# A windowed-attention and mixer kernel: the second period written out as a fixed list, and the global sums moved to the head of each period

## The chip, the cores and the metric

The kernel runs on one core of one Trainium2 chip. The time of a kernel is device microseconds (us) of one execution. TensorE (PE in the profile) multiplies matrices and writes to PSUM; VectorE (DVE) and ScalarE (ACT) read PSUM and do elementwise work; GpSimd (POOL) and SyncE (SP) issue transfers here, and GpSimd does some copies at the start. Every engine works through its own instructions strictly in the order in which the program lists them, and waits where an instruction needs something that is not ready.

## The reference, cut to what matters

For each of 8 batches, 8 heads of 576 positions and width 64 go through attention in which a position sees those within 32 of it and 8 global positions (and the global positions see all). The heads are joined to `x` (576 by 512), and a mixer follows: a token step and a channel step.

```
scores = where(|i - j| <= 32 or i global or j global, q @ k.T / 8, -1e9)
x = softmax(scores) @ v                        # heads joined: 8 x 576 x 512
u = x + (relu(x.T @ w_tok1) @ w_tok2).T        # 576 -> 256 -> 576
out = u + relu(u @ w_ch1) @ w_ch2              # 512 -> 1536 -> 512
```

## The kernel before

Batch 0's attention and token step stand at the start, written out instruction by instruction. After that comes a loop over b = 0 to 7. I call one turn a period. Period b does the channel step of batch b ("dense" work) and, between its parts, the attention and token step of the next batch, n = b + 1, and the first part of the attention of the batch after that, m = b + 2 ("sparse" work). The tile framework is in manual scheduling: each engine's order is the order in which the program calls the steps.

`dense(b)` is a list of units: 12 times `M4` (a channel product of four 128x512 matmuls into PSUM tile `b1p`, whose ReLU is taken by ScalarE at line 758), for odd b three `M4l` (`b1lp`: the last 64 rows of two batches together), and then `M5` in halves of six matmuls (`op`, line 781; VectorE adds the residual at line 785 into `osb`, and SyncE sends it out).

The sparse steps of a batch, with their names in the profile:

- `TR` and `t` = `T` + `TE`: transposes of q and k (`pr`, `pT`), copied out by VectorE (lines 438, 406, 412); one `T` for each of four head pairs. `globals_` copies the global queries (line 392).
- `s2(b, p)`: band scores of a head pair (`s`, line 458), exponentials by ScalarE (line 470); `SM`: masks on VectorE, first the eight global columns into `eg` (line 476), then the band (line 481, twice).
- `GK`: scores with the global queries (`gk`), exponentials (lines 527, 528), mask (`lf`, line 532).
- `OG`: the global positions' sums (`og`, line 539). It reads `eg` of all four head pairs, so it needs the first instruction of the last `SM`. VectorE copies it out as `rf` (line 544).
- `v_odd`: two copies on VectorE (`vod`, lines 373 and 374) of v shifted by 64 rows.
- `PV(b, tau)`: the output of attention for 128 positions (`pv`, lines 656 and 665); it begins with `rf`, and VectorE divides at lines 678 and 679 into `x`.
- `M1`: token product 1 (`a1p`), ReLU on ScalarE (line 700; batch 1: lines 697, 698); `M2`: token product 2 (`hp`), residual on VectorE (lines 721, 724) into `u` and `ul`; `M3`: transposes of `u` by DMA on SyncE's queue (`uT`), or, for batch 1, `M3p` on TensorE (`pu`, line 745; copied out at line 747). `uT` is what `M4` of that batch reads.
- `casts`: ten conversions of the loaded q and k of batch m on ScalarE (lines 383, 386), in pairs.

PSUM tiles come from three pools: `psm` (two buffers: `b1p`, `b1lp`, `op` and some of the transposes), `pss` (two larger buffers: scores, half of `pv`, `a1p`, `hp`) and `psv` (one large buffer: `gk`, `og`, the other `pv`). A new tile waits until the engine that reads the old one in its buffer is done.

The order of the two kinds of work is set in two ways. `play(steps, d)` runs a fixed list, in which an entry `D` stands for "the next dense unit". `merge(sparse, dense)` deals the two lists out by cost weights. Period 0 is a fixed list `period_0` (it ends, once its 20 dense units are used up, in a stretch of sparse steps alone: `M3p`, `M2(1, 2)`, and the first transposes and scores of batch 2). Period 1 is `merge(sparse2(), units)`. Periods 2 to 7 are `first_half(b)` with the `M4` units and `second_half(b)` with the `M5` units; `second_half` ends with `OG` of the next batch but one.

Of the kernel before, what the change touches and what calls it, by code (L numbers as in the profile page):

```python
# [9 lines left out]
F16 = mybir.dt.float16  # L10
# [5 lines left out]
P = 128  # L16
# [28 lines left out]
def kernel(  # L45
# [342 lines left out]
    def casts(b):  # L388
        return [lambda ti=ti, p=p: cast_qk(b, ti, p, nc.scalar.copy) for p in (None, 0, 1, 2, 3) for ti in range(2)]
# [4 lines left out]
        )  # L394

    def T(b, p):
        pT = (psm if b in (0, 2) else psv if b == 1 or p % 2 else pss)([P, 2, 512], F16, name=f"pT_{b}_{p}")
        for ti, n in enumerate((qn, kn)):
            for i in range(4):
                nc.tensor.transpose(  # L400
                    out=pT[:, ti, P * i : P * i + P], in_=n[b % 2][:, i, 2 * p : 2 * p + 2, :], identity=ident
                )
        st[b]["pT", p] = pT
# [15 lines left out]
        TEk(b, p)  # L419

    def TR(b):
        pr = (psm if b in (0, 2) else psv)([P, 2, 4, NP * 16], name=f"pr_{b}")
        sel = ident.rearrange("p (n r x) -> p r n x", n=NP, r=2)
        for ti, n in enumerate((qr, kr)):
            for i in range(4):
                for par in range(2):
                    nc.tensor.matmul(
                        pr[64 * par : 64 * par + 64, ti, i, :], lhsT=n[b % 2][:, i, :], rhs=sel[:, par], start=True, stop=True
                    )
        st[b]["pr"] = pr  # L430
        if b > 0:
            TRE(b)
# [74 lines left out]

    def GK(b):
        s = st[b]
        ps = (psv if b != 2 else pss)([P, 2, 512], name=f"gk_{b}")  # L510
        for p in range(NP):
            o = ps[32 * p : 32 * p + 32]
            qv = qTs[b % 2][:, p, :, NG:QS]
            w = kgz[:, b, p, :]
            nc.tensor.matmul(o[:, 0, 0:384], lhsT=w, rhs=qv[:, 0:3], start=True, stop=True)
            nc.tensor.matmul(o[:, 1, 0:128], lhsT=w, rhs=qv[:, 3], start=True, stop=True)
            nc.tensor.matmul(o[:, 1, 128:192], lhsT=w, rhs=qv[:, 4, 0:LAST], start=True, stop=True)
        s["gk"] = ps
# [14 lines left out]

    def OG(b):
        s = st[b]
        ps = (psv if b != 2 else pss)([P, 2, VW], name=f"og_{b}")
        for c in range(NT):
            for p in range(NP):
                nc.tensor.matmul(
                    ps[32 * p : 32 * p + 32], lhsT=eg[:, c, 2 * p : 2 * p + 2, :],  # L540
                    rhs=vsh[b % 2][:, c, 2 * p : 2 * p + 2, :], start=(c == 0), stop=(c == NT - 1),
                )
        rf = mb.tile([P, NP, 2, VW], F16, tag="rf", name=f"rf_{b}")
        nc.vector.tensor_tensor(
            out=rf, in0=ps.unsqueeze(1).to_broadcast([P, NP, 2, VW]),
            in1=blk.rearrange("p (n r) -> p n r", r=2).unsqueeze(3).to_broadcast([P, NP, 2, VW]), op=ALU.mult,
        )
        s["rf"] = rf
# [98 lines left out]
    def PV(b, tau):  # L647
# [145 lines left out]
        T(b, p)  # L793
        TE(b, p)

    def sparse2():
        b, n = 2, 3
        cs = casts(n)

        def cast(k):  # L800
            return [(0.0, c) for c in cs[2 * k : 2 * k + 2]]

        u = [(0.0, lambda: (load_rest(n), load_qk(n, slice(0, H))))]
        u += [(1.0, s2(b, 1)), (0.0, lambda: SM(b, 1)), (1.0, lambda: t(b, 3)), (1.5, s2(b, 2)), (0.0, lambda: SM(b, 2)), (0.0, lambda: v_odd(b))]
        u += [(0.3, lambda: GK(b)), (0.3, lambda: S_(b, 3, 0)), (1.8, lambda: S_(b, 3, 1)), (0.0, lambda: SM(b, 3))]
        u += [(2.5, lambda: OG(b))]
        u += [(2.0, lambda: PV(b, 0)), (2.0, lambda: PV(b, 1)), *cast(0), (2.0, lambda: PV(b, 2)), *cast(1)]
        u += [(0.0, lambda: PV(b, 3)), (1.0, lambda: [M1(b, ch) for ch in range(3)]), *cast(2)]
        u += [(2.0, lambda: PV(b, 4)), *cast(3), (3.0, lambda: [M1(b, ch) for ch in range(3, NT)]), *cast(4)]
        u += [(0.0, lambda: (load_rest(n + 1), load_qk(n + 1, slice(0, H))))]  # L810
        u += [(0.0, lambda: load_v16(n))]
        u += [(1.3, lambda: (M2(b, 0), M3(b, 0))), (1.0, lambda: (M2(b, 1), M3(b, 1)))]
        u += [(2.0, lambda: (M2(b, 2), M3(b, 2) if b % 2 else None))]
        u += [(1.0, lambda: (globals_(n), TR(n)))]
        u += [(1.2, lambda p=p: t(n, p)) for p in range(NP)]
        for p in range(NP):
            u += [(0.3, lambda p=p: S_(n, p, 0)), (2.2, lambda p=p: S_(n, p, 1)), (0.0, lambda p=p: SM(n, p))]
            if p == 2:
                u += [(0.5, lambda: GK(n)), (0.0, lambda: v_odd(n))]
        return u  # L820
# [14 lines left out]
    def period_0():  # L835
        n, m = 1, 2
        D = None
        c2 = casts(m)
        c1 = [lambda ti=ti, p=p: cast_qk(1, ti, p, nc.scalar.copy) for p in (2, 3) for ti in range(2)]
        u = [D, D, D, D, D, D, lambda: TR(n), lambda: globals_(n), D, lambda: t(n, 0), *c1[:2], D]  # L840
        u += [lambda: t(n, 1), *c1[2:], lambda: (load_qk1(2), load_v16(2)), D, s2(n, 0), D, lambda: t(n, 2), lambda: SM(n, 0), D, s2(n, 1), D]
        u += [lambda: t(n, 3), lambda: SM(n, 1), s2(n, 2), lambda: v_odd(n), D, lambda: SM(n, 2), lambda: GK(n), s2(n, 3), D]
        u += [lambda: SM(n, 3), lambda: OG(n), D, lambda: PV(n, 0), lambda: PV(n, 1), D, lambda: PV(n, 2), lambda: PV(n, 3), D]
        u += [*c2, lambda: PV(n, 4), lambda: [M1(n, ch) for ch in range(NT - 1)], D, lambda: M1(n, NT - 1), lambda: globals_(m), D]
        u += [lambda: M2(n, 0), lambda: M2(n, 1), lambda: TR(m), D, lambda: M3p(n, 0), lambda: t(m, 0)]
        u += [lambda: M3p(n, 1), lambda: (M2(n, 2), M3(n, 2)), lambda: t(m, 1)]
        u += [s2(m, 0), lambda: t(m, 2), lambda: SM(m, 0)]
        return u

        return u  # L850

    def first_half(b):
        n, m = b + 1, b + 2
        D = None
        cs = casts(m) if m < B else []

        def c(k):
            return cs[2 * k : 2 * k + 2]

        def tt(p):  # L860
            return [lambda: t(m, p)] if m < B else []

        def pv(tau):
            return lambda: PV(n, tau)

        if n == B:
            return []
        u = [D, *([lambda: OG(n)] if b == 2 else []), D, pv(0), pv(1), *c(0), D, *c(1), D, pv(2), pv(3), *c(2), D, lambda: [M1(n, ch) for ch in range(3)], D]
        if b == 2:
            u += [lambda: gather_t(1)]  # L870
        u += [pv(4), *c(3), D, lambda: M1(n, 3), D, *([lambda: TR(m)] if m < B else []), lambda: M1(n, 4), *c(4)]
        if m < B:
            u += [lambda: load_v16(m), lambda: globals_(m)]
        if m + 1 < B:
            u += [lambda: (load_rest(m + 1), load_qk(m + 1, slice(0, H)))]
        u += [D, *tt(0), D, lambda: (M2(n, 0), M3(n, 0)), D, *tt(1), lambda: (M2(n, 1), M3(n, 1)), D, *tt(2)]
        u += [lambda: (M2(n, 2), M3(n, 2) if n % 2 else None), D]
        return u

    def second_half(b):  # L880
        m = b + 2
        D = None
# [195 lines left out]
```

## Time and profile before

| | |
|---|---|
| median of 5 runs | 334.48 us (333.73 to 335.51) |
| the profiled execution | 332.79 us, its span from first to last instruction 330.7 us |
| TensorE clock granted, mean | 0.997 |
| busy: TensorE, VectorE, ScalarE, GpSimd | 310.9, 190.8, 155.2, 62.5 us |
| chain that ended last: share on TensorE, VectorE | 78%, 16% |

The shares are averages over stages that are bound by different things, and the end of a matmul in the profile is modelled. So the useful view is a stretch of the timeline, engine by engine, and what is read from it is start to start: the time from the start of one step to the start of the next. A bracket at the end of a line names the idle time of the engine ahead of it and who ended it. Period 0 begins at about 36 us, period 1 at about 78, period 2 at about 121, and the later ones follow every 35 to 38 us.

### The profile page before, as it was taken

How to read it: one execution, taken by the hardware profiler on the slowest of the kernel's cores; microseconds unless marked ns; L12 is line 12 of the kernel's file. 1: busy time of each engine (PE TensorE's matmuls, PEld its weight loads, DVE VectorE, ACT ScalarE, POOL GpSimd, SP SyncE). 2: the span in 40 equal slices, each digit the busy share in tenths (PEclk: the TensorE clock that was granted, in tenths of full speed). 3: DMA queues.
4: the chain of work that ended last, by engine and by line, in shares of the span. 5: the costliest groups of instructions: out<-in, count | busy, mean ns of one | idle time of the engine just before them, and what ended most of it. 6: DMA issues, size and time to landing. Idle time of an engine off the chain costs nothing.

```text
span 330.7 us, 8236 instructions
## 1 busy us (share of the span) xinstructions
PE 310.9 (94%) x3505; PEld 171.2 (52%) x3505; DVE 190.8 (58%) x414; ACT 155.2 (47%) x281; POOL 62.5 (19%) x95
## 2 busy tenths in 40 slices
PE   4999997997999999999999999999999999999994
PEld 4768544544455545454556445544556445444641
DVE  7378469669644875577736574577636574431021
ACT  3561685336665166625574326725673423504600
POOL 5796569410040004000310004000000000000000
PEclk9999999999999999999999999999999999999998
DMA  7899998995696919493589419593003111051012
GB/s 226 193 152 226 279 186 213 226 113 113 225 92 139 257 66 116 46 295 113 83 55 294 90 65 113 81 268 107 34 0 65 66 64 34 14 131 63 2 73 86
DMA packets 78198, 41.85 MB, mean 127 GB/s; under 512 B 54482, under 2 KB 72274, under 8 KB 78162
## 3 DMA queue, kind: packets, MB, share of 16 engines
q0 software_dynamic: 38608, 12.88, 32.1%
q1 hardware_dynamic: 39552, 28.45, 31.9%
q8 instruction: 27, 0.44, 0.5%
q14 instruction: 9, 0.07, 0.1%
q10 hardware_dynamic: 2, 0.00, 0.0%
HBM read 36.11 MB, written 9.44 MB: 138 GB/s over the span
## 4 chain that ended last, share of the span: by engine, by line
PE 78%; DVE 16%; ACT 2%; issue 2%; DVEq 0%; ACTq 0%
PE op L781 25%; PE b1p L755 22%; PE a1p L692 5%; PE hp L716 4%; PE pv L656 3%; PE b1lp L768 3%; PE pT L400 3%; PE s L458 3%; PE pv L665 3%; PE warm L208 2%; DVE vod L373 2%; DVE vod L374 2%; DVE e_all L481 2%; DVE kT L412 1%; DVE qT L406 1%
## 5 line engine op out<-in xcount | busy, mean ns | idle before, releaser
L755 PE MATMUL b1p<-uT,wc 128*128 128x512 f16 x384 | 94.9, 380 | 0.8 <-ACT b L758 0.6
L758 ACT ACTIVATE b<-b1p 128x512 f16<-128x512 f32 x96 | 57.0, 599 | 76.6 <-PE b1p L755 76.6
L781 PE MATMUL op<-wc,b 128*128 128x512 f16 x384 | 90.0, 380 | 0.0
L470 ACT ACTIVATE e_all<-s 128x544 f16<-128x544 f32 (+1 forms) x64 | 40.9, 685 | 38.4 <-issue 26.0
L755 PEld LDWEIGHTS <-wc 128*128 128x128 f16 x384 | 34.9, 98 | 39.8 <-issue 2.2
L781 PEld LDWEIGHTS <-b 128*128 128x128 f16 x384 | 35.1, 98 | 39.0
L361 POOL DMA_DIRECT2D vsh<-in_v_dram x35 | 29.7, 854 | 133.4 <-DVE rr L678 115.9
L785 DVE TENSOR_TENSOR osb<-u,op 128x512 f32<-128x512 f16 x32 | 21.9, 686 | 53.1 <-PE op L781 51.0
L678 DVE RECIPROCAL rr<-pv 128x8 f32<-128x8 f32 (+1 forms) x35 | 7.1, 203 | 30.9 <-PE pv L665 30.9
L679 DVE TENSOR_TENSOR x<-pv,rr 128x512 f16<-128x512 f32 (+1 forms) x35 | 24.2, 691 | 1.2
L481 DVE TENSOR_TENSOR e_all<-e_all,bandm 128x616 f16<-128x616 f16 x56 | 24.3, 475 | 1.0
L406 DVE COPY qT<-pT 128x512 f16<-128x512 f16 x30 | 20.5, 685 | 6.7 <-PE pT L400 6.2
L721 DVE TENSOR_TENSOR u<-x,hp 128x1024 f16<-128x1024 f16 x14 | 17.0, 1217 | 12.1 <-PE hp L716 12.1
L412 DVE COPY kT<-pT 128x512 f16<-128x512 f16 x30 | 20.4, 680 | 1.9 <-PE pT L400 1.4
L716 PE MATMUL hp<-a,w 128*128 128x512 f16 x72 | 19.1, 378 | 1.4 <-DVE u L721 1.3
L656 PE MATMUL pv<-rf,lf 128*64 128x264 f16 x126 | 18.3, 283 | 0.9 <-DVE kgz L355 0.7
L386 ACT CAST kn<-lk 128x512 f16<-128x512 f32 x27 | 16.8, 621 | 2.6 <-DMA lk<-in_k_dram 2.6
L665 PE MATMUL pv<-vsh,e_all 128*64 128x66 f16 x280 | 18.0, 194 | 0.0
L386 ACT CAST qn<-lq 128x512 f16<-128x512 f32 x27 | 16.5, 613 | 3.1 <-DMA lq<-in_q_dram 3.1
L665 PEld LDWEIGHTS <-e_all 128*64 128x64 f16 x504 | 17.9, 111 | 0.0
L458 PE MATMUL s<-qT,kT 64*64 64x136 f16 (+2 forms) x704 | 16.3, 216 | 1.2 <-DVE ul L724 0.7
L458 PEld LDWEIGHTS <-kT 64*64 64x64 f16 x704 | 10.8, 107 | 12.6 <-issue 10.9
(175 smaller groups left out, 354.2 us busy)
## 6 DMA issues: line engine op xcount, KB each, us to landing
out_dram<-osb SPq DMA_DIRECT2D x32, 256.0 KB
lq<-in_q_dram SPq DMA_DIRECT2D x5, 1024.0 KB
lk<-in_k_dram SPq DMA_DIRECT2D x5, 1024.0 KB
wc<-in_moe_w_ch_dram POOLq DMA_DIRECT2D x6, 512.0 KB, 13.5
vsh<-in_v_dram POOLq DMA_DIRECT2D x21, 128.0 KB, 4.5
lq<-in_q_dram POOLq DMA_DIRECT2D x2, 1024.0 KB
lk<-in_k_dram POOLq DMA_DIRECT2D x2, 1024.0 KB, 13.1
vsh<-in_v_dram POOLq DMA_DIRECT2D x14, 96.0 KB, 4.4
```

What stands on the lines that cost most here:

```text
L361: nc.gpsimd.dma_start(out=vsh[b % 2][r0:r1, c, :, 0:D], in_=v[b, :, j0 : j0 + (r1 - r0), :].rearrange("h p d -> p h d"),)
L386: eng(out=(qn, kn)[ti][b % 2][:, :, hs].rearrange("p i h d -> p h i d"), in_=(lq, lk)[ti][:, hs])
L458: nc.tensor.matmul(ps[o, par, i0 - a : i1 - a], lhsT=kT[r, HQ * j : HQ * j + HQ], rhs=qf[r, i0:i1], start=b > 0, stop=b > 0 or j in js[-2:],)
L470: nc.scalar.activation(out=e2[:, :, a:z], in_=ps[:, :, 0 : z - a], func=AF.Exp, scale=scale)
L481: nc.vector.tensor_mul(out=e2[:, par], in0=e2[:, par], in1=bm)
L656: nc.tensor.matmul(ps[r0 : r0 + 64, hf, 0 : NP * VW], lhsT=s["lf"][:, HQ * t : HQ * t + HQ], rhs=s["rf"][:, 2 * hf : 2 * hf + 2], start=Tr ...
L665: nc.tensor.matmul(ps[r0 : r0 + 64, hf, VW * hh : VW * hh + VW], lhsT=e_all[:, h, lo : lo + HQ], rhs=(vod if t % 2 else vsh)[b % 2][:, tau ...
L679: nc.vector.tensor_tensor(out=x16s[b % 2][r, tau, :].rearrange("p (f h x) -> p f h x", f=2, h=NP), in0=pq[r, :, :, 0:D], in1=rr[r].unsquee ...
L716: nc.tensor.matmul(ps[:, i, :], lhsT=w2[:, ch, P * tau - sh : P * tau - sh + P], rhs=s["a1"][:, ch, :], start=(ch == 0), stop=(ch == 1),)
L755: nc.tensor.matmul(ps, lhsT=wc1[:, cc, P * j : P * j + P], rhs=s["uT"][:, cc, :], start=(cc == 0), stop=(cc == 3))
L758: nc.scalar.activation(out=s["b1"][:, j, :], in_=ps, func=AF.Relu)
L781: nc.tensor.matmul(ps, lhsT=w, rhs=wc2[:, j, :], start=(j == 0), stop=(j == NJ - 1))
```

## The change

Period 1 becomes a fixed list, `period_1`, which begins after `M3p(1, 1)`: the last steps of `period_0` move into it, with channel products of batch 1 between them. `sparse2` goes. `OG` moves from the end of `second_half` to the head of `first_half`, behind one channel product. In `second_half`, `v_odd` moves from the place after `GK` to the place before the third `SM`; in `period_0`, from before the third `SM` to after the fourth. In `first_half` the casts and some dense units change places: in particular the token ReLU of `M1(n, 4)` now comes behind the last pair of casts, and one channel product fewer stands between `M1(n, 4)` and `M2(n, 0)`. Some PSUM tiles of batches 1 and 2 change pool.

```diff
     def T(b, p):
-        pT = (psm if b in (0, 2) else psv if b == 1 or p % 2 else pss)([P, 2, 512], F16, name=f"pT_{b}_{p}")
+        pT = (psm if b == 0 or (b, p) in ((2, 0), (2, 2), (1, 1)) else psv if b < 3 or p % 2 else pss)([P, 2, 512], F16, name=f"pT_{b}_{p}")
...
-        pr = (psm if b in (0, 2) else psv)([P, 2, 4, NP * 16], name=f"pr_{b}")
+        pr = (psm if b in (0, 2) else pss if b == 1 else psv)([P, 2, 4, NP * 16], name=f"pr_{b}")
...
-        ps = (psv if b != 2 else pss)([P, 2, 512], name=f"gk_{b}")
+        ps = psv([P, 2, 512], name=f"gk_{b}")
...
-        ps = (psv if b != 2 else pss)([P, 2, VW], name=f"og_{b}")
+        ps = psv([P, 2, VW], name=f"og_{b}")
...
-        ps = (pss if b != 2 and tau % 2 else psv)([P, 2, 512], name=f"pv_{b}_{tau}")
+        ps = (pss if tau % 2 else psv)([P, 2, 512], name=f"pv_{b}_{tau}")
...
-    def sparse2():
...
     def period_0():
...
-        u += [lambda: t(n, 3), lambda: SM(n, 1), s2(n, 2), lambda: v_odd(n), D, lambda: SM(n, 2), lambda: GK(n), s2(n, 3), D]
-        u += [lambda: SM(n, 3), lambda: OG(n), D, lambda: PV(n, 0), lambda: PV(n, 1), D, lambda: PV(n, 2), lambda: PV(n, 3), D]
+        u += [lambda: t(n, 3), lambda: SM(n, 1), s2(n, 2), D, lambda: SM(n, 2), lambda: GK(n), s2(n, 3), D]
+        u += [lambda: SM(n, 3), lambda: v_odd(n), lambda: OG(n), D, lambda: PV(n, 0), lambda: PV(n, 1), D, lambda: PV(n, 2), lambda: PV(n, 3), D]
...
-        u += [lambda: M3p(n, 1), lambda: (M2(n, 2), M3(n, 2)), lambda: t(m, 1)]
-        u += [s2(m, 0), lambda: t(m, 2), lambda: SM(m, 0)]
+        u += [lambda: M3p(n, 1)]
         return u
...
+    def period_1():
+        n, m = 2, 3
+        D = None
+        c3 = casts(m)
+        u = [D, lambda: (M2(1, 2), M3(1, 2)), D, lambda: t(n, 1), lambda: (load_rest(m), load_qk(m, slice(0, H))), D, s2(n, 0), D]
+        u += [lambda: t(n, 2), lambda: SM(n, 0), D, s2(n, 1), D, lambda: t(n, 3), lambda: SM(n, 1), D, s2(n, 2), lambda: v_odd(n), D]
+        u += [lambda: SM(n, 2), lambda: GK(n), D, s2(n, 3), D, lambda: SM(n, 3), lambda: OG(n), *c3[0:2], D, D, lambda: PV(n, 0)]
+        u += [lambda: PV(n, 1), *c3[2:4], D, *c3[4:6], D, lambda: PV(n, 2), lambda: PV(n, 3), *c3[6:8], D]
+        u += [lambda: [M1(n, ch) for ch in range(3)], *c3[8:10], D, lambda: PV(n, 4), lambda: load_v16(m), D, lambda: M1(n, 3)]
+        u += [lambda: TR(m), lambda: M1(n, 4), lambda: (load_rest(m + 1), load_qk(m + 1, slice(0, H))), lambda: globals_(m), D, lambda: t(m, 0), D]
+        u += [lambda: (M2(n, 0), M3(n, 0)), D, lambda: t(m, 1), lambda: (M2(n, 1), M3(n, 1)), D, lambda: t(m, 2), D, lambda: M2(n, 2)]
+        u += [lambda: t(m, 3), s2(m, 0), D, lambda: SM(m, 0), s2(m, 1), D, lambda: SM(m, 1), s2(m, 2), D, lambda: SM(m, 2), lambda: GK(m)]
+        u += [D, s2(m, 3), lambda: v_odd(m), lambda: SM(m, 3), D]
         return u
...
     def first_half(b):
...
-        u = [D, *([lambda: OG(n)] if b == 2 else []), D, pv(0), pv(1), *c(0), D, *c(1), D, pv(2), pv(3), *c(2), D, lambda: [M1(n, ch) for ch in range(3)], D]
+        u = [D, lambda: OG(n), *c(0), D, D, pv(0), pv(1), *c(1), D, *c(2), D, pv(2), pv(3), D, lambda: [M1(n, ch) for ch in range(3)], *c(3), D]
         if b == 2:
             u += [lambda: gather_t(1)]
-        u += [pv(4), *c(3), D, lambda: M1(n, 3), D, *([lambda: TR(m)] if m < B else []), lambda: M1(n, 4), *c(4)]
+        u += [pv(4), D, lambda: M1(n, 3), *c(4), D, *([lambda: TR(m)] if m < B else []), lambda: M1(n, 4)]
...
-        u += [D, *tt(0), D, lambda: (M2(n, 0), M3(n, 0)), D, *tt(1), lambda: (M2(n, 1), M3(n, 1)), D, *tt(2)]
-        u += [lambda: (M2(n, 2), M3(n, 2) if n % 2 else None), D]
+        u += [*tt(0), D, lambda: (M2(n, 0), M3(n, 0)), D, *tt(1), lambda: (M2(n, 1), M3(n, 1)), D]
+        u += [*tt(2), lambda: (M2(n, 2), M3(n, 2) if n % 2 else None)]
         return u

     def second_half(b):
...
-        return [D, s2(m, 0), D, lambda: t(m, 3), lambda: SM(m, 0), D, s2(m, 1), D, lambda: SM(m, 1), D, s2(m, 2), D,
-                lambda: SM(m, 2), lambda: GK(m), lambda: v_odd(m), s2(m, 3), D, lambda: SM(m, 3), D, lambda: OG(m)]
+        return [D, s2(m, 0), D, lambda: t(m, 3), D, lambda: SM(m, 0), s2(m, 1), D, lambda: SM(m, 1), D, s2(m, 2), lambda: v_odd(m), D, lambda: SM(m, 2),
+                lambda: GK(m), s2(m, 3), D, lambda: SM(m, 3), D]
...
         if b == 1:
-            merge(sparse2(), units)
+            play(period_1(), units)
             continue
```

More of the change, by code (lines that the diff above doesn't have):

```diff
@@ L794, in t @@
         TE(b, p)
-    def sparse2():
[L797 to L820, printed above, removed]
     def play(steps, d):
@@ L841, in period_0 @@
         u += [lambda: t(n, 1), *c1[2:], lambda: (load_qk1(2), load_v16(2)), D, s2(n, 0), D, lambda: t(n, 2), lambda: SM(n, 0), D, s2(n, 1), D]
-        u += [lambda: t(n, 3), lambda: SM(n, 1), s2(n, 2), lambda: v_odd(n), D, lambda: SM(n, 2), lambda: GK(n), s2(n, 3), D]
-        u += [lambda: SM(n, 3), lambda: OG(n), D, lambda: PV(n, 0), lambda: PV(n, 1), D, lambda: PV(n, 2), lambda: PV(n, 3), D]
+        u += [lambda: t(n, 3), lambda: SM(n, 1), s2(n, 2), D, lambda: SM(n, 2), lambda: GK(n), s2(n, 3), D]
+        u += [lambda: SM(n, 3), lambda: v_odd(n), lambda: OG(n), D, lambda: PV(n, 0), lambda: PV(n, 1), D, lambda: PV(n, 2), lambda: PV(n, 3), D]
         u += [*c2, lambda: PV(n, 4), lambda: [M1(n, ch) for ch in range(NT - 1)], D, lambda: M1(n, NT - 1), lambda: globals_(m), D]
         u += [lambda: M2(n, 0), lambda: M2(n, 1), lambda: TR(m), D, lambda: M3p(n, 0), lambda: t(m, 0)]
-        u += [lambda: M3p(n, 1), lambda: (M2(n, 2), M3(n, 2)), lambda: t(m, 1)]
-        u += [s2(m, 0), lambda: t(m, 2), lambda: SM(m, 0)]
-        return u
+        u += [lambda: M3p(n, 1)]
+        return u
+        return u
+    def period_1():
[11 more added lines that the diff above has]
+        u += [D, s2(m, 3), lambda: v_odd(m), lambda: SM(m, 3), D]
         return u
```

## The prediction

> **What bounds the kernel now.** I read the page's first two parts, then TensorE's waits, then the timeline of each period engine by engine.
>
> ```profile
> PE 310.9 (94%) x3505; PEld 171.2 (52%) x3505; DVE 190.8 (58%) x414; ACT 155.2 (47%) x281; POOL 62.5 (19%) x95
> ...
> PEclk9999999999999999999999999999999999999998
> ```
>
> TensorE sets the pace and has its full clock everywhere. The change leaves its work alone (as many matmuls, in another order), so it can only win or lose TensorE's waits and the turn between kinds of tile. Its listed waits are few:
>
> ```profile
> PE og L539 <- DVE eg L476: 2.6, 3, 1.7
> ...
> PE hp L716 <- DVE u L721: 1.3, 4, 0.3
> PE s L458 <- DVE ul L724: 0.7, 1, 0.7
> ...
> PE b1p L755 <- ACT b L758: 0.6, 2, 0.4
> ```
>
> Modelled matmul ends hide more, so I take start to start. Full-speed prices from undisturbed places: M4 0.86 us, an op half 1.29, M4l 0.90, T 0.45, s2 0.40 and GK 0.38 (each 0.1 more behind a wide matmul), OG 0.46, two PV in a row 1.19, one alone 0.70, M1 0.43 a step, M2 0.86, 0.86 and 0.43. What a reader needs of the lags: a reader of PSUM starts about 0.2 behind the last matmul (0.27 for the token ReLU), TensorE 0.06 behind the reader's end.
>
> The join of two periods shows where TensorE waits although no bracket says so. VectorE and TensorE at the end of period 2:
>
> ```profile
> 151.65 0.87 DVE L481 TENSOR_TENSOR e_all<-e_all,bandm 128x616 f16<-128x616 f16 x2
> 153.91 0.69 DVE L785 TENSOR_TENSOR osb<-u,op 128x512 f32<-128x512 f16 x1 [1.39 <-PE op L781]
> ...
> 156.01 0.71 DVE L373 COPY vod<-vsh 64x2112 f16<-64x2112 f16 x1
> 156.75 0.70 DVE L374 COPY vod<-vsh 64x2112 f16<-64x2112 f16 x1
> 157.37 0.18 DVE L476 TENSOR_TENSOR eg<-e_all,egm 128x80 f16<-128x80 f16 x1
> ...
> 158.38 0.68 DVE L785 TENSOR_TENSOR osb<-u,op 128x512 f32<-128x512 f16 x1
> ```
>
> ```profile
> 157.27 0.80 PE L539 MATMUL og<-vsh,eg 128*32 128x132 f16 x20
> 158.00 2.13 PE L755 MATMUL b1p<-uT,wc 128*128 128x512 f16 x8
> 160.06 0.30 PE L656 MATMUL pv<-rf,lf 128*64 128x264 f16 x2
> ```
>
> OG holds TensorE for 0.73 instead of 0.46, because eg comes at 157.55 behind the v copy. The two channel products take 2.06 instead of 1.82, because the second needs the buffer that osb frees at 159.06. And VectorE had idled 1.39 us earlier.
>
> **The change part by part.**
>
> *Batch 1's pools (period 0).* pT_1 waited 0.61 for pT_0's copy; in psm it doesn't, but the next M4 then waits for the ReLU of M4 number 7, done at 44.68: it starts at 44.75 instead of 44.94. Gain 0.19. pr in pss costs nothing: that pool is free until the first scores.
>
> *v copy of batch 1 behind the last masks.* Before, VectorE is full from 50.48 on:
>
> ```profile
> 52.81 0.71 DVE L373 COPY vod<-vsh 64x2112 f16<-64x2112 f16 x1
> 53.55 0.95 DVE L374 COPY vod<-vsh 64x2112 f16<-64x2112 f16 x1
> ...
> 55.80 0.68 DVE L785 TENSOR_TENSOR osb<-u,op 128x512 f32<-128x512 f16 x1
> 56.39 0.19 DVE L476 TENSOR_TENSOR eg<-e_all,egm 128x80 f16<-128x80 f16 x1
> ...
> 57.41 0.70 DVE L544 TENSOR_TENSOR rf<-og,blk 128x528 f16<-128x528 f32 x1
> ```
>
> Without the copy (1.6 us) the masks come earlier, but osb needs op, whose end is at 54.23, and starts only at 54.45. So: osb to 55.05, eg at 55.24, masks to 56.07, copy to 57.5, rf to 58.2. OG no longer waits 1.75; PV waits for rf instead and starts at 58.26 (58.43 before). What is late next: the casts of batch 2, behind lk's landing, hold ScalarE until the token ReLU starts at 67.81, whatever TensorE does:
>
> ```profile
> 67.29 0.61 ACT L386 CAST kn<-lk 128x512 f16<-128x512 f32 x1
> 67.81 0.59 ACT L697 ACTIVATE a<-a1p 128x512 f16<-128x512 f32 x1
> ```
>
> So both edits end here: between 0 and 0.2 gained; I take 0.
>
> Here a rule speaks against the change. The copies now stand at 56.1 to 57.5, among five v loads that GpSimd issues from 54.00 to 58.30. The row: a copy beside GpSimd's issuing took 0.71 (52.81) and 0.95 (53.55), against 0.70 with GpSimd idle (156.75), so 0.25 more at most. The Trainium skill (SBUF — State Buffer, Who interferes with whom) says that a two-port copy on VectorE and GpSimd lock each other out of a shared pair of ports for a whole instruction. By the row PV starts up to 0.25 later and the cast limit swallows most. By the rule the copy could be shut out until 58.30: rf at 60.4, PV 2.0 later, about 1.85 lost. I take the row; the rule sets the far end.
>
> *The head of period 1.* M4 number 0 now stands right behind pu and reads all of uT. VectorE copies the last part of it at 75.46 to 75.88, behind q and k of pT_0, so TensorE waits from 74.64 to 75.95: 1.31. Before, M2, T and half of s2 filled this.
>
> I carried period 1 on by hand in this manner, queue by queue. Other waits of the new list: M4 number 4, 0.68 (its buffer's ReLU queues behind a pair of exponentials that ends at 81.24); OG of batch 2, 0.82 (exponentials of the last scores end at 90.1, eg follows); s2 of batch 3, 0.20 (ul); OG of batch 3, 1.99. The last is fixed by VectorE: from the end of the last op half, 0.22 + osb 0.60 + SM 1.02 + mask 0.48 + v copy 1.36 + eg 0.18 + 0.06 = 3.9 us, while TensorE has only GK, s2 and one M4 (1.8). Sum 5.00. The same reckoning of the old list, with its waits read from the trace (0.73, 0.50, 0.50, 0.29, 0.35, 0.17, 0.17, 0.14, 0.05, 0.73, 0.17): 3.80. The new list saves turns: four single PV become two pairs, 2.80 to 2.38; three scores are no longer split, 0.12 each. Net +1.20 - 0.42 - 0.36 = +0.42. It isn't seen in the trace, so it has ends: -2.5 (half of the new waits don't come) and +2.
>
> Hidden in it: SyncE sends q and k of batch 4 and out ahead of uT of batch 2. The loads' bytes flow about 7 us behind their issue (102.9 before, 105.3 now), and transposes follow: done at 114.3 before, 116.7 now by the same 11.4. M4 of period 2 comes at 120.5. The 3.8 us between are the cover; each us beyond costs one. q and k of batch 3 are issued some 1.5 us later and land by 90; casts start at 90.5. GpSimd's v loads wait for PV as before, a period ahead.
>
> *Joins of periods 2 to 5.* The v copy (1.45) fits into VectorE's idle 1.39 before osb, which moves 0.1. eg and osb come early, OG stands behind an M4: 0.27 saved at four joins, 0.24 at the two even ones (behind an odd period the last op tile leaves room). Sum -1.56. If a v copy still delayed osb there, TensorE wouldn't feel it: op's buffer has 3 us.
>
> *Token ReLU in first_half.* The row of period 6, which has no sparse work to hide in:
>
> ```profile
> 283.18 0.59 PE L692 MATMUL a1p<-x,w1l 128*128 128x512 f16 x2
> 283.87 1.02 ACT L700 ACTIVATE a<-a1p 128x1024 f16<-128x1024 f32 x1
> 285.33 1.03 PE L716 MATMUL hp<-a,w 128*128 128x512 f16 x4
> ```
>
> From the end of a1p the ReLU takes 0.27 + 1.02 + 0.06 = 1.35. Before, two M4 (1.73) covered it. Now one M4 (0.86): 0.49, say 0.50, lost in period 6. In periods 2 to 5, T and M4 (1.31) cover it: 0.04 each, 0.16. The casts ahead of it end in time (ScalarE is free at 3.09 after M4 number 7 starts, a1p's lag ends at 3.32).
>
> *Nothing:* the 0.3 waits of hp for u stay, their order is the same; gather_t stays next to PV; periods 6 and 7 beyond the ReLU are unchanged.
>
> **Sum:** 0 + 0.42 - 1.56 + 0.50 + 0.16 = -0.48, say -0.5. The profiled execution (332.79, of which the span is 330.7 and 2.1 lie around it) would be 332.3; it ran 1.7 under the median, so I put the change onto the median: 334.0.
>
> **The rivals.** What a measurement tells from no change is about 0.3%, 1.0 us.
>
> - A, forecast: waits change places, 334.0, own range 333.2 to 334.6. Chance 0.46, of which 0.10 lies beyond -1.0.
> - B, faster: the fixed list avoids half its 5.0 us of new waits, -0.5 - 2.5 = 331.5. For it: ScalarE has 0.5 to 1 us to spare between most of its steps. Against it: the 1.31 and the 1.99 follow from VectorE's order alone. 0.24.
> - C, slower: the port lock at batch 1's v copy, +1.85 - 0.48 = 335.85. Place: 56.1 us; it decides from a delay of 1.6 on (0.1 swallowed by the casts, 0.5 by the gain elsewhere, 1.0 to count). Against it: 0.71 and 0.95 in the row. 0.15.
> - D, slower: in period 1 a ReLU behind exponentials holds M4 not once but at each of the four score pairs, 3 x 0.68 more: 336.0. Against it: 1.0 us of margin at the other three. 0.10.
> - E: the change doesn't do what it says, since uT's transposes land late and period 2 waits; at 5.5 us late, 335.7. 0.05.
>
> Faster: 0.10 + 0.24 = 0.34. Same: 0.36, from A. Slower: C, D and E, 0.30. The range takes in B's centre and A, and reaches C: 331.5 to 335.8.
>
> **What would show it.** In the profile after: no wait of 1.7 at og near 55, but PV right behind rf at 58.2 to 58.5; a wait of 1.3 at the first b1p at 75.9; og near 121.4 cut by 2 us; OG at the later joins 0.46 long behind a b1p, v copies in VectorE's former gap; hp in period 6 waiting 0.5 for ScalarE. Wrong it would be if periods 2 to 5 don't shorten by 0.3 to 0.5 each, or if period 1 takes over 1 us more or less.

## The result, and the profile after

The changed kernel took 334.09 us (median of 42 runs, 331.85 to 338.47), the kernel before 335.06 us (79 runs beside them). The ratio is 0.9975, with a 95% interval of 0.9958 to 0.9991: faster by 0.84 us, of which the interval allows 0.3 to 1.4. The forecast was 334.0, a gain of 0.48. (Ratios leave disturbed runs out; the medians given with the experiments hold all runs, so the two need not agree to the last tenth.)

The profiled execution took 331.87 us, its span is 330.1. I first look at the page's busy times and at TensorE's waits, to compare them with those shown of before:

```profile
PE 308.3 (93%) x3505; PEld 170.7 (52%) x3505; DVE 192.3 (58%) x414; ACT 155.7 (47%) x281; POOL 62.3 (19%) x95
...
PEclk9999999999999999999999999999999999999998
```

```profile
PE og L539 <- DVE eg L476: 3.1, 3, 1.8
...
PE hp L716 <- DVE u L721: 1.3, 4, 0.3
PE pv L656 <- DVE rf L544: 1.2, 1, 1.2
PE b1p L755 <- DVE uT L747: 1.1, 1, 1.1
PE b1p L755 <- ACT b L758: 1.0, 2, 0.5
...
PE hp L716 <- ACT a L700: 0.3, 1, 0.3
```

As many instructions on every engine, the same clock. The list of waits has become longer, not shorter, although the time is less: `b1p` now waits for `uT`, `pv` for `rf`, `hp` for the token ReLU, and `og` waits more. All four were named ahead of the result. What the list can't show is what went away, since it stood in no bracket. For that the stages are needed.

I cut the timeline of TensorE into stages, start to start. *Period 0* runs from the first `b1p` to the second `pu` of batch 1, *period 1* to the first `pv` of batch 3, *periods 2 to 5* to the first `pv` of batch 7, *period 6* to the first `hp` of batch 7. The new `first_half` has one M4 more ahead of a `pv`, so for kernels with it I take 0.86 from period 1 and add it to period 6. Behind the last stage TensorE has some 40.5 us more to do in every kernel.

| kernel | first `b1p` at | period 0 | period 1 | periods 2 to 5 | period 6 |
|---|---|---|---|---|---|
| before | 35.79 | 38.41 | 50.68 | 148.39 | 12.06 |
| after | 37.07 | 38.02 | 50.67 | 146.49 | 12.52 |
| difference | +1.28 | -0.39 | -0.01 | -1.90 | +0.46 |
| e1_joins | 37.02 | 38.45 | 50.54 | 146.49 | 12.52 |
| e2_list | 36.52 | 38.76 | 51.79 | 148.83 | 12.06 |
| e3_vcopy | 37.83 | 38.71 | 50.68 | 148.41 | 12.06 |
| e4_v_early | 36.21 | 39.31 | 49.54 | 146.50 | 12.53 |
| e5_relu6 | 37.56 | 38.13 | 52.35 | 146.49 | 12.05 |
| e6_head | 35.90 | 38.72 | 49.83 | 146.51 | 12.52 |
| e7_all_waits | 37.03 | 38.23 | 48.01 | 146.49 | 12.05 |
| e8_hp_late | 37.32 | 38.54 | 48.00 | 144.51 | 12.05 |
| e9_buffers | 39.22 | 37.99 | 46.62 | 144.52 | 12.05 |

Rows e5 and e2 hold a fall of the granted clock, and period 0 of e1 to e4 and e6 a score pair that stood longer; both are told below. The gain comes from the joins of periods 2 to 5. At the join whose waiting was shown of before, TensorE's timeline of after reads:

```profile
158.08 1.03 PE L755 MATMUL b1p<-uT,wc 128*128 128x512 f16 x4
159.04 0.47 PE L539 MATMUL og<-vsh,eg 128*32 128x132 f16 x20
159.44 1.90 PE L755 MATMUL b1p<-uT,wc 128*128 128x512 f16 x8
161.27 0.30 PE L656 MATMUL pv<-rf,lf 128*64 128x264 f16 x2
```

and VectorE's:

```profile
151.72 0.69 DVE L785 TENSOR_TENSOR osb<-u,op 128x512 f32<-128x512 f16 x1 [0.64 <-PE op L781]
...
153.45 0.71 DVE L373 COPY vod<-vsh 64x2112 f16<-64x2112 f16 x1
154.19 0.70 DVE L374 COPY vod<-vsh 64x2112 f16<-64x2112 f16 x1
154.82 0.68 DVE L785 TENSOR_TENSOR osb<-u,op 128x512 f32<-128x512 f16 x1
...
157.13 0.20 DVE L476 TENSOR_TENSOR eg<-e_all,egm 128x80 f16<-128x80 f16 x1 [0.26 <-ACT e_all L470]
```

OG now holds TensorE for 159.44 - 159.04 = 0.40 (0.73 before), and the two channel products for 1.83 (2.06 before). The v copies lie in the gap in which VectorE had idled for 1.39, and eg comes as soon as the exponentials allow, 1.7 us and more ahead of need.

### The profile page after: what moved, and what is told of

Its sections match the earlier page's. It is cut to its first block, busy times and chain, and to the rows that moved or that the text cites. A ratio compares the mean times of both kernels' runs of the same rounds, so it can differ in the third digit from the quotient of the medians.

```text
span 330.1 us, 8234 instructions
## 1 busy us (share of the span) xinstructions
PE 308.3 (93%) x3505; PEld 170.7 (52%) x3505; DVE 192.3 (58%) x414; ACT 155.7 (47%) x281; POOL 62.3 (19%) x95
## 4 chain that ended last, share of the span: by engine, by line
PE 74%; DMA 12%; DVE 6%; SPq 3%; ACT 2%; issue 1%; POOL 1%; POOLq 0%; ACTq 0%
PE op L781 28%; PE b1p L755 21%; DMA wc<-in_moe_w_ch_dram 8%; PE a1p L692 5%; PE hp L716 4%; PE b1lp L768 3%; PE pv L656 3%; PE pv L665 3%; PE s L458 3%; PE pT L400 2%; DMA lq<-in_q_dram 2%; DMA lk<-in_k_dram 2%; DVE u L721 1%; DMA lv<-in_v_dram 1%; SPq L128 1%
## 5 line engine op out<-in xcount | busy, mean ns | idle before, releaser
L470 ACT ACTIVATE e_all<-s 128x544 f16<-128x544 f32 (+1 forms) x64 | 40.5, 687 | 35.5 <-issue 16.4
```

The source lines that it names most:

```text
L470: nc.scalar.activation(out=e2[:, :, a:z], in_=ps[:, :, 0 : z - a], func=AF.Exp, scale=scale)
```

## The experiments

**e1_joins: the halves alone.** The kernel before, with `first_half` and `second_half` of after; `period_0`, the merged period 1 and the pools stay.

```diff
-        u = [D, *([lambda: OG(n)] if b == 2 else []), D, pv(0), pv(1), *c(0), D, *c(1), D, pv(2), pv(3), *c(2), D, lambda: [M1(n, ch) for ch in range(3)], D]
+        u = [D, lambda: OG(n), *c(0), D, D, pv(0), pv(1), *c(1), D, *c(2), D, pv(2), pv(3), D, lambda: [M1(n, ch) for ch in range(3)], *c(3), D]
...
```

> Only first_half and second_half of the change (periods 2 to 7): OG at the head of the period, v copy ahead of the third masks, the new places of the casts. Theory A (the joins carry the gain): from the first PV of batch 3 to the first PV of batch 7 it takes 146.5 us as in the changed kernel (148.39 before), from there to token product 2 of batch 7 11.66 (12.06 with one M4 more before), period 0 and the period after it stay as before within 0.3; time 1.4 under before. Rival L (the fixed list of period 1 carries it): that stretch stays at 148.4 and the time at before's. Rival S (the gain is in period 0, where the v copy of batch 1 moved): time as before.

Measured: 335.03 us against 334.87, ratio 0.9962 (0.9928 to 0.9997). Periods 2 to 5 take 146.49, exactly as in after, and period 6 takes 12.52: the two effects belong to these functions and to nothing else. Period 1 is within 0.14 of before.

**e2_list: the list alone.** The other half: after, with `first_half` and `second_half` of before, and batch 1's v copy at its old place.

```diff
-        u = [D, lambda: OG(n), *c(0), D, D, pv(0), pv(1), *c(1), D, *c(2), D, pv(2), pv(3), D, lambda: [M1(n, ch) for ch in range(3)], *c(3), D]
+        u = [D, *([lambda: OG(n)] if b == 2 else []), D, pv(0), pv(1), *c(0), D, *c(1), D, pv(2), pv(3), *c(2), D, lambda: [M1(n, ch) for ch in range(3)], D]
...
```

> Only period_1 with its pools (batch 1's too) and the shortened period_0; v copy of batch 1 and periods 2 to 7 as before. Theory A: waits in period 1 only change places: from the second pu of batch 1 to the first PV of batch 3 50.7 us plus or minus 0.3 (50.68 before), TensorE waits 1.3 at the first M4, 0.7 at M4 number 4, 0.7 and about 2.0 at the two OG; periods 2 to 7 as before; time as before within 0.5. Rival L: that stretch shortens by 1 us or more, time 1 us under before. The reckoning of the prediction said 0.4 longer.

Measured: 335.94, ratio 1.0006 (0.9975 to 1.0036): the list is worth nothing by itself. In its profiled execution period 1 is 1.11 longer than before and periods 2 to 5 are 0.44 longer. Before one believes that, the clock must be looked at. TensorE at OG of batch 3, and the table by windows (each with its length, the busy times of TensorE, its weight loads, VectorE, ScalarE and GpSimd, then the granted clock, DMA share and GB/s):

```profile
124.59 0.73 PE L539 MATMUL og<-vsh,eg 128*32 128x132 f16 x17 [1.83 <-DVE eg L476]
125.25 1.89 PE L755 MATMUL b1p<-uT,wc 128*128 128x512 f16 x4
```

```profile
121.21:124.62 3.41, 1.58 (x35) 0.71 (x37) 3.28 (x9) 2.35 (x5) 0.00 (x0) 1.00 0.36 82
124.62:128.03 3.41, 3.41 (x43) 1.73 (x45) 1.44 (x3) 0.86 (x3) 0.00 (x0) 0.50 0.00 0
```

One M4 took 1.89 instead of 1.03: behind the long wait for eg the granted clock was 0.50 for 3.41 us. That costs 3.41 x 0.50 = 1.7 us, and the two excesses are 1.55 together. Without the fall, the list is as long as the old one to within 0.2.

**e3_vcopy: batch 1's v copy alone.** The kernel before, with `v_odd(1)` moved behind the last masks.

```diff
-        u += [lambda: t(n, 3), lambda: SM(n, 1), s2(n, 2), lambda: v_odd(n), D, lambda: SM(n, 2), lambda: GK(n), s2(n, 3), D]
-        u += [lambda: SM(n, 3), lambda: OG(n), D, lambda: PV(n, 0), lambda: PV(n, 1), D, lambda: PV(n, 2), lambda: PV(n, 3), D]
+        u += [lambda: t(n, 3), lambda: SM(n, 1), s2(n, 2), D, lambda: SM(n, 2), lambda: GK(n), s2(n, 3), D]
+        u += [lambda: SM(n, 3), lambda: v_odd(n), lambda: OG(n), D, lambda: PV(n, 0), lambda: PV(n, 1), D, lambda: PV(n, 2), lambda: PV(n, 3), D]
```

> Only the v copy of batch 1 moved behind the last masks, all else as before. Theory A: OG waits 0.6 to 0.8 in place of 1.75, PV waits 1.0 to 1.2 for rf, and the stretch from the first M4 to the second pu of batch 1 changes by 0 to -0.2 (38.41 before; 38.02 in the changed kernel, whose transposes also sit in other pools). Rival S: it shortens by the whole 0.39. Rival K (a lock between GpSimd's issuing and the copy): the copies take over 1 us each and the stretch grows by 1 to 1.9.

Measured: one run, 335.09. OG's wait falls to 0.72, `pv` waits 1.39 for `rf` instead, and period 0 takes 38.71 (38.41 before), outside the 0 to -0.2 of theory A. But 0.25 of the 0.30 is a score pair that stood longer ahead of OG (see e4_v_early). OG and the op half behind it take 4.21 instead of 4.09, start to start: the wait changed its place and grew a little, and the first of the two copies took 0.97 beside GpSimd's v loads.

**e4_v_early: the longest wait of the list.** After, with `v_odd(3)` moved from between the last masks to a place after `M1(2, 3)`.

```diff
-        u += [lambda: TR(m), lambda: M1(n, 4), lambda: (load_rest(m + 1), load_qk(m + 1, slice(0, H))), lambda: globals_(m), D, lambda: t(m, 0), D]
+        u += [lambda: v_odd(m), lambda: TR(m), lambda: M1(n, 4), lambda: (load_rest(m + 1), load_qk(m + 1, slice(0, H))), lambda: globals_(m), D, lambda: t(m, 0), D]
...
-        u += [D, s2(m, 3), lambda: v_odd(m), lambda: SM(m, 3), D]
+        u += [D, s2(m, 3), lambda: SM(m, 3), D]
```

> The changed kernel with one move: the v copy of batch 3 from between the last masks to between M1(2, 3) and TR(3), where VectorE idles 1.4 us. Theory A (OG of batch 3 waits for VectorE's chain osb, masks, mask, v copy, eg): its wait falls from 2.0 to 0.8 or 0.9, where the exponentials of the last scores become the limit, and the stretch from the second pu to the first PV of batch 3 falls from 51.53 to 50.4; time 1.1 under the changed kernel. Rival X (the wait is ScalarE's exponentials): wait and time stay.

Measured: 333.28, ratio 0.9964 (0.9936 to 0.9992). Period 1 falls by 1.13. TensorE and VectorE at OG of batch 3:

```profile
123.70 0.46 PE L539 MATMUL og<-vsh,eg 128*32 128x132 f16 x17 [0.70 <-DVE eg L476]
```

```profile
123.44 0.20 DVE L476 TENSOR_TENSOR eg<-e_all,egm 128x80 f16<-128x80 f16 x1 [0.25 <-ACT e_all L470]
```

VectorE's order made the wait, as the prediction had worked out; with the copy gone from it, VectorE itself waits, and ScalarE's exponentials set the 0.70 that is left. In the time less is seen than the 1.1 expected: among runs with a mean granted clock of 0.995 or more, after has a median of 332.43 (12 runs) and e4 of 332.10 (10 runs).

The profiled execution may hold a reason. Its period 0 is 1.03 longer than the list explains: a score pair takes 1.43 instead of 0.40. TensorE and ScalarE there:

```profile
51.73 0.34 PE L458 MATMUL s<-qT,kT 64*64 64x72 f16 x12 [0.84 <-ACT e_all L470]
```

```profile
50.93 0.74 ACT L470 ACTIVATE e_all<-s 128x688 f16<-128x688 f32 x1 [0.93 <-PE s L458]
```

The scores that this exponential reads were done by 49.22, and the clock is full. The same pair takes 1.02, 1.78 and 0.65 in e1, e2 and e3, and an earlier pair 0.58 in e6. Behind a pair that stands, OG's wait shrinks in turn, so only part of it is left in period 0 of e1 and e2. The cause stays open, and whether the pair stands in the runs without a profile is not shown.

**e5_relu6: the token ReLU's cover in period 6.** After, with the M4 between `M1(7, 3)` and `M1(7, 4)` put behind the latter.

```diff
-        u += [pv(4), D, lambda: M1(n, 3), *c(4), D, *([lambda: TR(m)] if m < B else []), lambda: M1(n, 4)]
+        u += [pv(4), D, lambda: M1(n, 3), *c(4), *([D, lambda: TR(m)] if m < B else []), lambda: M1(n, 4), *([] if m < B else [D])]
```

> The kernel after, with the two M4 of period 6 put back between the token MLP's last a1p product and its hp product (one of them taken from in front of M1(n,3)); periods 2 to 5 as in after. The prediction's step says that one M4 (0.86) leaves 0.49 of the ReLU's 1.35 uncovered. If so, the stretch from the first PV of batch 7 to its first hp, 11.66 us in after with one M4 less in it (12.06 before), becomes 12.06 (one M4 of 0.86 moves into it, 0.46 of waiting goes), the wait of hp for ACT a (0.3) is gone, and the last stage, 40.46, shortens by 0.86; 0.46 less in all. Rival: the 0.46 is the turn between kinds of tile, and does not go; then 12.52.

The expectation has an error: the M4 moves inside the stretch, so its number there doesn't change, and "0.46 less" means 11.66 to 11.20. Measured: 11.19 (12.05 in the table), the rest unchanged.

```profile
284.85 1.89 PE L755 MATMUL b1p<-uT,wc 128*128 128x512 f16 x8
286.58 1.03 PE L716 MATMUL hp<-a,w 128*128 128x512 f16 x4
```

`hp` follows the two M4 with no bracket. The single run took 334.04, and period 1 took 1.68 more than in after: here too the clock fell, to 0.50 from 77.77 to 81.18 us, right behind the wait for `uT` at the head of the list (3.41 x 0.50 = 1.7).

**e6_head: the head of period 1.** After, with token product 2 and a transpose of q and k ahead of the first M4.

```diff
-        pT = (psm if b == 0 or (b, p) in ((2, 0), (2, 2), (1, 1)) else psv if b < 3 or p % 2 else pss)([P, 2, 512], F16, name=f"pT_{b}_{p}")
+        pT = (pss if (b, p) == (2, 1) else psm if b == 0 or (b, p) in ((2, 0), (2, 2), (1, 1)) else psv if b < 3 or p % 2 else pss)([P, 2, 512], F16, name=f"pT_{b}_{p}")
...
-        u = [D, lambda: (M2(1, 2), M3(1, 2)), D, lambda: t(n, 1), lambda: (load_rest(m), load_qk(m, slice(0, H))), D, s2(n, 0), D]
+        u = [lambda: (M2(1, 2), M3(1, 2)), lambda: t(n, 1), lambda: (load_rest(m), load_qk(m, slice(0, H))), D, D, D, s2(n, 0), D]
```

> The kernel after, with M2(1,2) and T(2,1) (its tile moved to the pool of the scores) ahead of the first M4 of period 1, and that M4's two companions directly before s2(2,0); as many products in all. If the 1.30 of waiting at the first M4 (75.53 to 76.83 in after) is VectorE's copy of uT and nothing else, 0.43 + 0.45 of other work covers it: a wait of 0.3 to 0.5 stays, and the stage from the second pu to the first PV of batch 3 falls from 51.53 by 0.8 to 1.0. Rival: what the head gains is given back by the later steps, since T(2,1)'s copies hold VectorE and the ReLU of M4 number 3 or 4 waits behind exponentials instead; then less than 0.3 is left.

Measured: one run, 330.88; period 1 is 0.84 shorter. TensorE's timeline:

```profile
75.06 0.59 PE L716 MATMUL hp<-a,w 128*128 128x512 f16 x2
...
75.72 0.39 PE L400 MATMUL pT<-ident,kn 128*128 128x128 f16 x4
76.36 2.79 PE L755 MATMUL b1p<-uT,wc 128*128 128x512 f16 x12 [0.25 <-DVE uT L747]
```

A bracket of 0.25 is left of 1.13, and nothing of the gain is given back later.

**e7_all_waits.** e4, e5 and e6 together, and OG of batch 2 behind the first of the two M4 that followed it.

```diff
-        u += [lambda: SM(n, 2), lambda: GK(n), D, s2(n, 3), D, lambda: SM(n, 3), lambda: OG(n), *c3[0:2], D, D, lambda: PV(n, 0)]
+        u += [lambda: SM(n, 2), lambda: GK(n), D, s2(n, 3), D, lambda: SM(n, 3), D, lambda: OG(n), *c3[0:2], D, lambda: PV(n, 0)]
```

> e4_v_early with the head of e6_head, the cover of e5_relu6 in period 6, and OG of batch 2 behind one of the two M4 that follow it. If the 5.0 us of new waits in period 1 are each due to the engine that the prediction named, the stage of period 1 goes from 50.40 (e4_v_early) to 48.9 (0.9 at the head, 0.6 at OG of batch 2), the last two stages lose 0.46 together, and the whole is 2.0 us shorter than e4_v_early, about 2.8 to 3 us (0.9%) shorter than before. Rival: waits change places inside the list; then the stage stays above 49.8 and the time within 0.3% of e4_v_early.

Measured: 329.39, ratio 0.986 (0.9779 to 0.994). The stage that was expected at 48.9 took 48.87 (48.01 in the table). The waits don't change places here; 2.66 us of them go (51.53 to 48.87).

**e8_hp_late.** e7, with `M2(n, 2)` of batches 3 to 6 moved from the end of `first_half` into `second_half`.

```diff
-        u += [*tt(2), lambda: (M2(n, 2), M3(n, 2) if n % 2 else None)]
+        u += [*tt(2)]
+        if m >= B:
+            u += [lambda: (M2(n, 2), M3(n, 2) if n % 2 else None)]
...
-        return [D, s2(m, 0), D, lambda: t(m, 3), D, lambda: SM(m, 0), s2(m, 1), D, lambda: SM(m, 1), D, s2(m, 2), lambda: v_odd(m), D, lambda: SM(m, 2),
+        return [D, lambda: (M2(n, 2), M3(n, 2) if n % 2 else None), D, s2(m, 0), lambda: t(m, 3), D, lambda: SM(m, 0), s2(m, 1), D, lambda: SM(m, 1), D, s2(m, 2), lambda: v_odd(m), D, lambda: SM(m, 2),
...
```

> e7_all_waits with M2(n,2) of batches 3 to 6 behind the next M4 (and the score pair that followed behind the next op half), so that hp number 2 no longer waits for the addition of hp number 0. If the four waits of hp for u (0.33 each) are pure loss, periods 2 to 5 shorten by 0.33 each, 1.3 in all, 146.5 to 145.2. Rival: the addition of hp number 2 then stands later on VectorE, between masks and copies, and the scores or OG wait for it instead: 0 or a loss of up to 0.5 a period.

Measured: 328.15, ratio 0.981 (0.9721 to 0.9899). Each of the periods 2 to 5 is 0.49 shorter, not 0.33: the brackets had been too small. In after, start to start, the transpose ahead of that `hp` takes 0.94 in period 2, and an undisturbed one takes 0.45.

**e9_buffers.** e8, with T(2, 2) in the pool of one buffer, and OG of batch 3 behind two M4.

```diff
-        pT = (pss if (b, p) == (2, 1) else psm if b == 0 or (b, p) in ((2, 0), (2, 2), (1, 1)) else psv if b < 3 or p % 2 else pss)([P, 2, 512], F16, name=f"pT_{b}_{p}")
+        pT = (pss if (b, p) == (2, 1) else psm if b == 0 or (b, p) in ((2, 0), (1, 1)) else psv if b < 3 or p % 2 else pss)([P, 2, 512], F16, name=f"pT_{b}_{p}")
...
-        u = [D, lambda: OG(n), *c(0), D, D, pv(0), pv(1), *c(1), D, *c(2), D, pv(2), pv(3), D, lambda: [M1(n, ch) for ch in range(3)], *c(3), D]
+        u = [D, *([D] if b == 2 else []), lambda: OG(n), *c(0), D, *([] if b == 2 else [D]), pv(0), pv(1), *c(1), D, *c(2), D, pv(2), pv(3), D, lambda: [M1(n, ch) for ch in range(3)], *c(3), D]
```

> e8_hp_late with two more edits in period 1. T(2,2)'s tile lies in the pool of one buffer (psv) instead of in that of the M4, so M4 number 4 takes the buffer that M4 number 2 has left, and not that of number 3, whose ReLU stands behind exponentials: its wait of 0.67 should go, down to 0.1. And OG of batch 3 stands behind two M4 and in front of one (it stood behind one, in front of two): of its 0.70 of waiting for the exponentials and eg nothing is left, and PV waits 0.1 to 0.2 for rf, since one M4 (0.86) doesn't quite cover 0.2 + 0.70 + 0.06. Expected: the stage from the second pu to the first PV of batch 3 falls from 48.86 by 1.1 to 1.2, to 47.7, the rest as in e8_hp_late. Rival: T(2,3), which uses the same one buffer, waits for T(2,2)'s copies, and the next exponentials and M4 move with it: then at least 0.4 of the 0.6 comes back there.

Measured: 327.96, ratio 0.9763 (0.9709 to 0.9817), 1.8 to 2.9% under before and the lowest median here (that it is 0.19 under e8 is less than the spread of either; the stage tells them apart). Period 1 took 47.48 (46.62 in the table), 1.38 less than in e8:

```profile
83.39 1.03 PE L755 MATMUL b1p<-uT,wc 128*128 128x512 f16 x4
...
123.09 0.54 PE L539 MATMUL og<-vsh,eg 128*32 128x132 f16 x20
123.56 1.04 PE L755 MATMUL b1p<-uT,wc 128*128 128x512 f16 x4
124.69 0.30 PE L656 MATMUL pv<-rf,lf 128*64 128x264 f16 x2
```

M4 number 4 has no bracket, OG holds TensorE for 0.47, and the next M4 for 1.13 (0.86 and 0.27 of waiting for rf). From after to here period 1 has lost 4.05 us of waiting (51.53 to 47.48) with the same products; what had held them were places in VectorE's and ScalarE's queues, and one buffer.

## Why the prediction was right, and where its steps were not

The forecast was A, that waits change places, and so it was: the list is worth nothing, the joins pay, period 6 gives part of it back. That 334.0 stands so near to 334.09 is luck in part. The stages gave 1.84 where the sum had 0.48, and every term erred to the same side; the clock, which the prediction had at full rate everywhere, took some 0.7 of it back; and the forecast was put onto a median of 334.48, where the later runs of before have 335.06. By its steps:

*Period 1, forecast +0.42, measured -0.01.* Four of the five new waits, in after's TensorE timeline:

```profile
76.83 1.02 PE L755 MATMUL b1p<-uT,wc 128*128 128x512 f16 x4 [1.13 <-DVE uT L747]
...
82.78 1.02 PE L755 MATMUL b1p<-uT,wc 128*128 128x512 f16 x4 [0.52 <-ACT b L758]
...
91.29 0.46 PE L539 MATMUL og<-vsh,eg 128*32 128x132 f16 x17 [0.57 <-DVE eg L476]
...
124.39 0.46 PE L539 MATMUL og<-vsh,eg 128*32 128x132 f16 x17 [1.83 <-DVE eg L476]
```

Start to start, with 0.40 for OG itself (what it takes where nothing holds it, as at 159.04 above), they are 1.30, 0.68, 0.80, 0.27 (the score pair behind `ul`) and 2.06, 5.11 in all; the prediction had 1.31, 0.68, 0.82, 0.20 and 1.99, 5.00 (its working for the last, 3.9 against 1.8, gives 2.1). So the queue-by-queue working was good. The mis-sized term is the other one, the old list's waits, of which several were read from brackets, or against a price of OG (0.46) that already held a turn. TensorE before, at the largest two:

```profile
75.61 0.31 PE L458 MATMUL s<-qT,kT 64*64 64x72 f16 x10
76.66 0.34 PE L458 MATMUL s<-qT,kT 64*64 64x72 f16 x12 [0.73 <-DVE ul L724]
76.94 0.40 PE L400 MATMUL pT<-ident,qn 128*128 128x128 f16 x4
...
122.43 0.24 PE L539 MATMUL og<-vsh,eg 128*32 128x132 f16 x3
123.36 0.46 PE L539 MATMUL og<-vsh,eg 128*32 128x132 f16 x17 [0.69 <-DVE eg L476]
123.75 1.04 PE L755 MATMUL b1p<-uT,wc 128*128 128x512 f16 x4
```

A score pair and OG take 0.40 each undisturbed; here they take 1.33 and 1.32, so the waits are 0.93 and 0.92 where the sum had 0.73 and 0.73. Taken alike all through, the old list's waits are 4.32 and not 3.80. Then waiting grew by 0.79 and not by 1.20, and what is left, the saved turns, is 0.80, close to the 0.78 forecast.

*Joins, forecast -1.56, and ReLU in periods 2 to 5, forecast +0.16: measured -1.90 together.* OG gave 0.33 at each join, not 0.27 (the same turn again: OG behind a wide product takes 0.40, and 0.10 stands in the product ahead of it, before as after). The second product gave 0.23 at even joins and also 0.06 at odd ones, where the sum had none. 4 x 0.33 + 2 x 0.23 + 2 x 0.06 = 1.90. Of the ReLU's 0.16 hardly anything is there: in period 2 the M4 that covers it takes 0.89 instead of 0.86, in period 3 0.86.

*Period 6, forecast +0.50, measured +0.46.* ScalarE and TensorE, one timeline of each:

```profile
283.70 1.02 ACT L700 ACTIVATE a<-a1p 128x1024 f16<-128x1024 f32 x1
```

```profile
283.00 0.59 PE L692 MATMUL a1p<-x,w1l 128*128 128x512 f16 x2
283.44 1.03 PE L755 MATMUL b1p<-uT,wc 128*128 128x512 f16 x4
284.77 1.02 PE L716 MATMUL hp<-a,w 128*128 128x512 f16 x4 [0.30 <-ACT a L700]
```

One M4 between them, 1.33 from its start to `hp`: the wait is where the prediction put it.

*Period 0, forecast 0: -0.39 in this execution, but for other reasons than given.* The chain was: the pools give 0.19, OG's wait goes, `pv` waits for `rf`, and the casts swallow the rest. All but the last held. The pools of batch 1 gave 0.22 (M4 number 8 starts earlier and then waits for the ReLU, as worked out; 0.05 comes from the first transposes, where the sum had nothing), and OG with the op half behind it takes 3.99 instead of 4.09. TensorE, VectorE and ScalarE of after:

```profile
56.37 0.46 PE L539 MATMUL og<-vsh,eg 128*32 128x132 f16 x17 [0.72 <-DVE eg L476]
...
59.39 0.30 PE L656 MATMUL pv<-rf,lf 128*64 128x264 f16 x2 [1.16 <-DVE rf L544]
```

```profile
57.25 0.74 DVE L373 COPY vod<-vsh 64x2112 f16<-64x2112 f16 x1
58.02 0.70 DVE L374 COPY vod<-vsh 64x2112 f16<-64x2112 f16 x1
58.65 0.69 DVE L544 TENSOR_TENSOR rf<-og,blk 128x528 f16<-128x528 f32 x1
```

```profile
68.69 0.60 ACT L697 ACTIVATE a<-a1p 128x512 f16<-128x512 f32 x1 [2.84 <-PE a1p L692]
```

The casts swallowed nothing. The last line shows ScalarE idle for 2.84 ahead of the token ReLU; in the execution shown of before the casts had held the ReLU by 0.07, since lk had landed late (the missing 0.07 of the 0.39), and I took one transfer's landing for a property of the kernel. What else sets period 0 is how long the two v copies take. This was the disputed row. Where GpSimd issues no v load beside them, they take 0.71 and 0.70 (e9_buffers). Beside them, GpSimd and VectorE of e8_hp_late:

```profile
54.65 4.36 POOL L361 DMA_DIRECT2D vsh<-in_v_dram  x5
```

```profile
57.51 1.12 DVE L373 COPY vod<-vsh 64x2112 f16<-64x2112 f16 x1
58.66 0.85 DVE L374 COPY vod<-vsh 64x2112 f16<-64x2112 f16 x1
```

Their sums over the executions with the new period 0 are 1.41 (e9), 1.44 (after), 1.55 (e5), 1.66 (e7), 1.70 (e4), 1.97 (e8) and 1.97 (e6). Period 0 takes 37.99, 38.02, 38.13, 38.23, 38.28, 38.54 and 38.54, once the longer score pair is taken off in e4 (1.03) and e6 (0.18): each tenth of the copies goes through to the end of the period. So by the copies the edit brings -0.4 to +0.1, by the luck of when GpSimd issues its loads. The Trainium skill (SBUF — State Buffer, Who interferes with whom) is right that the two disturb each other. But no copy was shut out for the block of five loads: 0.41 was the most that one copy lost, about half of one load's issuing (4.36 / 5 = 0.87). The row was nearer than the far end (1.85), yet at up to 0.56 the loss was twice the 0.25 that I took from it. The row had been read too widely: its first copy ended at 53.52, before the v loads, and its second met them for its last half microsecond alone. Rival C didn't happen in any execution.

*Rivals B, D and E.* B needed half of the new waits away: all came. D needed the ReLU's hold at four places of period 1: it came at one. E needed late transposes: the first products of period 2 wait for none. But E was nearer than reckoned. SyncE's queue, before and after:

```profile
103.94 7.49 SPq L733 DMA_TRANSPOSE uT<-u  x4
```

```profile
110.54 7.67 SPq L733 DMA_TRANSPOSE uT<-u  x4
```

The transposes moved by 6.6 us, where the prediction had 2.4. If they are done as much later as they are issued, that is at 120.9 (the prediction's 114.3 and 6.6), and the first M4 of period 2 starts at 121.36: by this estimate 0.5 is left of the 3.8 us of cover.

*From the stages to the median.* The differences of after's row add to -1.84 (of which 0.39 lies in period 0), the ratio gave -0.84. The clock accounts for much of it, though this is a correlation and not an experiment. Among runs with a mean granted clock of 0.995 or more, before has a median of 333.99 (35 runs, those beside the first four experiments) and after of 332.43 (12 runs): 1.56 apart. The mean clocks lie in groups about 0.005 apart, as one fall of 3.41 us to half makes it (1.7 of 331 us). In the next group, 0.991 to 0.993, before has 335.66 (4 runs) and after 334.09 (18 runs): 1.57 apart, and both 1.7 above the first group. So at a like clock the change gives 1.56, and after is more often in a lower group. Runs of the first group are 35 of 59 for before, 11 of 22 for e1 and 10 of 22 for e4, and only 12 of 42 for after and 5 of 22 for e2, the two that have both long waits, 1.30 and 2.06. In two profiles (e2, e5) the clock fell right behind such a wait, and each fall cost 1.7. The prediction priced a wait at its own length.

## What to carry to other kernels

Read old and new waits by the same measure, start to start: brackets against modelled ends missed 0.17 in each `hp` and all of the joins' loss. For each moved step, ask which queue sets its wait, and then whether two or three steps that need nothing from that queue can stand in front: here seven such edits (e4 to e9) took 6.5 us from the stages behind period 0, beyond the 1.4 of the change itself. And fill a long wait before a short one: it may cost the clock as well as its own length.

## What I had not expected of the hardware

- The granted clock of TensorE fell to 0.50 for 3.41 us behind waits of only 2.0 us (e2, from 124.62) and 1.3 us (e5, from 77.77, with a wait of 0.5 for `pu` just ahead), and not in other executions with the same waits. The traces suggest why. The falls begin 116.05 and 68.27 us behind the trace's first record of the full clock, 34 and 20 times 3.413, and the stretch of this length just ahead of each is the emptiest between that record and the last products: TensorE is busy for 1.58 and 1.77 us of it. In after, the wait of 1.83 is divided between two such stretches (2.64 and 2.37 busy), and the one with the wait of 1.13 has 2.28. So where a wait lies against these stretches seems to decide. A limit can't be read from it: e8 has one with 1.73 and no fall, and e9 fell at 28.86, for twice 3.41, behind one with 2.58 of small products. The Trainium skill (TensorE: Matmul & The Clock Gate, What's actually happening) tells of half rate after an idle window of about 3.4 us, and of a window that runs free, so that the moment varies. The length and the free running agree; but the stretches ahead of these falls were about half busy, not idle.
- The prologue, the same code in all kernels, ends between 35.79 and 39.22 us, a spread of four times the measured gain. In e9 (39.22) the clock was at 0.50 from 28.86 to 35.69 us; for the others I have no cause.
- A copy on VectorE that takes 0.70 alone took 0.71 to 1.12 beside GpSimd's issuing of transfers.
